# A pooled-attention and shrink kernel: order of loads, stores and last tokens on the queues, and the engine that places the turned keys, in groups 3 to 6

## The chip, the cores and the metric

One core of a Trainium2 chip. The metric is the time of one execution on the device, in microseconds (us). The kernel before takes 295.48 us as the median of three runs (294.96 to 295.68).

## The reference

Queries, keys and values are 8 batches x 8 heads x 576 tokens x 64. Keys and values are averaged over 8 neighbouring tokens, so that each head has 72 pooled keys. Each token's attention output goes, all heads side by side, through a two-layer block of width 512, 2048, 512.

```python
k_p = k.reshape(B, H, Sp, pool, D).mean(axis=3)
v_p = v.reshape(B, H, Sp, pool, D).mean(axis=3)
scores = scale * np.matmul(q, k_p.transpose(0, 1, 3, 2))
scores = scores - np.max(scores, axis=-1, keepdims=True)
attn = np.exp(scores)
attn = attn / (np.sum(attn, axis=-1, keepdims=True) + 1e-09)
attn_out = np.matmul(attn, v_p)
x = attn_out.transpose(0, 2, 1, 3).reshape(B * S, H * D)
h = x @ w_in
out = (h - np.tanh(h)) @ w_out
```

## The kernel before

**Tiling.** The 4608 tokens are worked on in nine groups of 512. Groups 0 to 7 are the first 512 tokens of batches 0 to 7. The last 64 tokens of each batch are gathered, two batches at a time, into four "tail" units, which together make group 8. While the two-layer block of group `g` runs, the attention of batch `nb = g + 1` is woven into it, and the loading and pooling for batch `nb + 1 = g + 2`.

**A group from 3 on** (`SEVEN`) has two stages. In the h stage TensorE multiplies by `w_in` into pairs of PSUM banks (`h_mms`, L445). ScalarE takes the tanh of a pair (L458) and VectorE subtracts it (L459, into `gT`); there are eight pairs. In the products stage the second multiplication is done by seven block products in place of eight (`product`, L591), for 14 steps `u` = 0 to 13. The operand of the third product, `S3`, is a VectorE difference of parts of `gT` (`g_sum`, L573), done in two halves at the end of the h stage. TensorE needs it at step u = 4. VectorE and GpSimd make the other sums (L573, L623, L624, L628), ScalarE and VectorE empty PSUM.

**The attention of the next batch** is placed by the table `PLAN7`: "s" are scores (`s_mms`, L311) with the maximum and the subtraction on VectorE (L323, L326), "e" the exponential on ScalarE (L362), "t" the turning of two units' exponentials by a transposing DMA (`e_turn_dma`, L371, into `ET`), "a" the values (`av_mms`, L398) and the normalising on VectorE (L419, L420), "x" the turning of the result into the next group's `xT` (L428). Keys -16 to -1 are steps of the h stage, keys from 0 on are the steps `u`. A tail's scores stand at u = 9.

**Preparation of the batch after.** GpSimd pools the values of batch `nb` (`pool_v`, L229 to L256), then the keys of batch `nb + 1` (`pool_k`, L214 to L220) at the start of a group. ScalarE casts its queries (`q_cast`, L280). `seven_more(u)` then issues on the SP queue the turning of the queries at u = 0 (`q_turn_dma`, L286) and of the keys at u = 7 (`k_turn_dma`, L272), the loading of a tail's queries at u = 7 when `nb` is even (`tail_pieces`, L176), and at u = 13 the placing of the turned keys into `KB` by GpSimd (`k_place_kT`, two copies at L266), the cast of the tail's queries by GpSimd (`tail_cast`, L184) and the loads of keys and queries of batch `g + 3` (`load_for`, L136, L142, L164). `KB` is read by the first scores of the next group. The tail's queries are turned (`turn_tail`, L187) behind the first "t" of the next group.

**Order on a queue.** Each engine, and SP with it, takes its instructions in the order of the program; semaphores make an instruction wait for what it depends on. SP issues nearly all DMAs from group 1 on, the transposing ones too. A half of a group's output is stored by `store_half` (L632): half 1 at u = 11, behind a GpSimd sum (`finish_22`, L628), half 0 at u = 13, so half 1 stands ahead of the loads on SP and half 0 behind them.

In the lines below `se` is ScalarE's copy and `ge` GpSimd's.

Of the kernel before, what the change touches and what calls it, by code (L numbers as in the profile page):

```python
# [38 lines left out]
def kernel(  # L39
# [130 lines left out]
    def run(pieces, n=16):  # L170
        for _ in range(min(n, len(pieces))):
            pieces.pop(0)()

    def tail_pieces(i, eng=None):
        return [
            lambda s=s: (eng or nc.sync).dma_start(  # L176
                out=tl_raw[64 * s : 64 * s + 64, :, :],
                in_=q[2 * i + s, :, QA:S, :].rearrange("h p d -> p h d"),
            )
            for s in range(2)  # L180
        ]

    def tail_cast(i):
        nc.gpsimd.tensor_copy(out=tl_bf[i % 2][:, :, :], in_=tl_raw[:, :, :])  # L184
# [737 lines left out]
        9: [("sb", 4, P45)],  # L922
        11: [("e", 4), ("t", 2)],
    }
    late, carry = [], []

    def tail_values(i):
        av_mms(slot_tl, av_tail(i), P67)
# [6 lines left out]
    for g in range(1, NG):  # L935
        nb = g + 1 if g + 1 < B else None
        more = nb is not None and nb + 1 < B

        tail = {2: 0, 3: 1, 5: 2, 7: 3}.get(nb)
        plan = {}  # L940
        if nb is not None:
            units = [(s_block(nb, j), av_block(nb), slot(4 * nb + j)) for j in range(4)]
            s_pairs, a_pairs = [0, 0, 0, 1, 2], [0, 1, 0, 2, 1]
            plan = {
                -12: [("s", 0)],
                -9: [("e", 0)],
                -8: [("s", 1)],
                -5: [("e", 1), ("t", 0)],
                -3: [("s", 2)],
                0: [("e", 2)],  # L950
                1: [("s", 3)],
                3: [("e", 3), ("t", 1)],
                4: [("a", 0)],
                5: [("a", 1), ("x", 0)],
                9: [("a", 2), ("a", 3), ("x", 1)],
            }
            if g == 1:
                plan[-10], plan[-7], plan[-5] = plan.pop(-12), plan.pop(-9), plan.pop(-8)
                plan[-2], plan[-1] = [("e", 1), ("t", 0)], plan.pop(-3)
            if tail is not None:  # L960
                units.append((s_tail(tail), av_tail(tail), slot_tl))
                plan[3].append(("s", 4))
                plan[4] += [("e", 4), ("t", 2)]
                if g == 1:
                    plan[6], plan[7] = plan[4][:1], plan.pop(5)
                    plan[4] = plan[4][1:]
                    plan[10] = plan.pop(9)
                plan[12] = [("a", 4), ("x", 2)]
            if g in SEVEN:
                plan = {u: its for u, its in PLAN7.items() if tail is not None or u < 9}  # L970
            xs = [x_pair(), x_pair(), x_tl]
        if nb is not None:
            pool_v(nb, nc.gpsimd)
        if more and g in SEVEN:
            pool_k(nb + 1, nc.gpsimd)
        shs = {}

        def seven_more(u):
            if u == 0:
                q_turn_dma(nb + 1)  # L980
            if u == 7:
                k_turn_dma(nb + 1)
                if nb % 2 == 0:
                    run(tail_pieces(nb // 2))
            if u == 13:
                k_place_kT(nb + 1, ge)
                if nb % 2 == 0:
                    tail_cast(nb // 2)
                load_for(g + 1)

        def step(kind, n, bk=None):
            if kind == "t2":
                e_turn_dma(units[2][2], n, n + 1)
                return
            if kind == "t":
                e_turn_dma(units[2 * n][2], 0, 2 if n < 2 else 1)
                if tail and n == 0:
                    turn_tail(tail)
                return
            if kind == "x":  # L1000
                x_turn_dma(xs[n], *((nb, 2 * n, 2) if n < 2 else (B, tail, 1)))
                return
            s, a, sl = units[n]
            if kind == "s" and bk:
                s_mms(s, bk)
                ng = s_max(bk)
                late.append(lambda: s_exp_heads(bk, ng, sl))
            elif kind in ("s", "sb"):
                bk = bk or PAIRS[s_pairs[n]]
                s_mms(s, bk)  # L1010
                shs[n] = s_shift(bk)
            elif kind == "e":
                s_exp(shs[n], sl)
            else:
                bk = bk or PAIRS[a_pairs[n]]
                av_mms(sl, a, bk)
                normalise(bk, xs[n // 2][:, n % 2, :, :, :])

        for i in range(NHID):
            bk = HB[i // 2 % 3][i % 2] if g in SEVEN else i % 6  # L1020
            h_mms(g, i, bk)
            if g in SEVEN and i == 15:
                for it in plan.pop(-1, ()):
                    step(*it)
            if i % 2:
                h_act(i - 1, bk - 1)
                if g in SEVEN:
                    if nb is None and i in (3, 5) and carry:
                        carry.pop(0)()
                    for n, i0 in {13: [(3, 0)], 15: [(3, 4)]}.get(i, ()):  # L1030
                        g_sum(n, i0, i0 + 4)
                    if i == 15 and nb is None:
                        for n in (2, 1):
                            g_sum(n, 0, NQ)
            for it in plan.get(i - NHID, ()):
                step(*it)
            if more and i in (13, 15):
                q_cast(nb + 1, se, i - 13, i - 11)
        v_next = v_pieces(nb + 1) if more else []
        if g > 1:  # L1040
            run(v_next)
        for u in range(14 if g in SEVEN else 0):
            n, b = PRODUCTS[u // 2], u % 2
            product(n, b)
            evacuate(n, b, nb is not None)
            for it in plan.get(u, ()):
                step(*it)
                run_late()
            if nb is not None and u in (9, 10) and carry:
                carry.pop(0)()  # L1050
            if more:
                seven_more(u)
            if nb is not None and u == 2:
                dep = g_sum(2, 0, NQ)
                after([g_sum(1, 0, 4, nc.gpsimd), g_sum(1, 4, NQ, nc.gpsimd)], dep)
            if u == (3 if nb is None else 8):
                g_sum(4, 0, NQ)
            if g == NG - 1:
                if n == "1" and b:
                    finish_11(nc.vector)  # L1060
                    store_part(0, C1, 0, 2)
                elif n == "6" and b:
                    store_part(1, C1, 0, 2)
                elif n == "5" and b:
                    store_part(1, C2, 0, 2, (nc.sync, nc.scalar))
                elif n == "3":
                    store_part(0, C2, b, b + 1, (nc.sync, nc.scalar))
            elif b:
                if n == "1":
                    finish_11(nc.gpsimd, nb is not None)  # L1070
                elif n in "53":
                    if n == "5" and nb is not None:
                        finish_22(nc.gpsimd)
                    store_half(g, 0 if n == "3" else 1)
        if g in SEVEN and tail is not None:
            carry += [lambda i=tail: tail_values(i), lambda i=tail: x_turn_dma(x_tl, B, i, 1)]
        for u, (tb, qd) in enumerate(() if g in SEVEN else UNITS):
            o_mms(tb, qd * 4, qd * 4 + 4, 4 + tb % 2)
            if qd == 3:
                o_store(g, tb, 4 + tb % 2, se)  # L1080
                if g == 1 or tb > 1:
                    run(stores)
            for it in plan.get(u, ()):
                step(*it)
            if u == 0 and more:
                pool_k(nb + 1, nc.gpsimd)
            if more:
                if u == (0 if g == 1 else 3):
                    q_turn_dma(nb + 1)
                if u == 0:  # L1090
                    run(stores)
                if u == (4 if g == 1 else 9):
                    k_turn_dma(nb + 1)
                    k_place_kT(nb + 1, ge)
                if u == 11 and nb % 2 == 0:
                    run(tail_pieces(nb // 2))
                    tail_cast(nb // 2)
            if u == 13:
                load_for(g + 1)
            if u in (8, 9, 13, 14):  # L1100
                w_ops.pop(0)()
# [29 lines left out]
```

## Time and profile before

| what | value |
|---|---|
| median of three runs | 295.48 us |
| the profiled execution's own time | 294.32 us |
| its span in the profile | 292.6 us |
| TensorE busy | 280.9 us, 96% of the span |
| VectorE busy | 222.0 us, 76% |
| GpSimd busy | 153.0 us, 52% |
| ScalarE busy | 147.4 us, 50% |
| granted TensorE clock | 1.0 throughout |

PE is the matmul side of TensorE, PEld its weight loads, DVE is VectorE, ACT ScalarE, POOL GpSimd. SPq stands for instructions that SP issues to the DMA queue. A busy sum of TensorE is an average over the whole span; what a stage can win is read from its waits. Groups 3 to 6 begin at 116.65, 145.46, 175.82 and 206.0 us of the span, group 7 at 235.32 us.

### The profile page before, as it was taken

The numbers are of one execution on the slowest core, as the hardware profiler recorded it, in microseconds if no ns is written. First come the engines' busy times: TensorE is split into PE (matmuls) and PEld (weight loads), VectorE is DVE, ScalarE is ACT, GpSimd is POOL, SyncE is SP. The second block draws the span as 40 slices with busy tenths as digits, with TensorE's granted clock in tenths as the row PEclk, the third lists the DMA queues.
The fourth block names the chain that finished last, engine by engine and source line by source line (L and its number), as shares of the span: only waits on it lengthen the run. The fifth ranks groups of instructions, "written<-read, shape, count | busy, mean of one in ns | idle before, by whom it ended". The sixth has DMA issues, their size and how long they took to land.

```text
span 292.6 us, 5473 instructions
## 1 busy us (share of the span) xinstructions
PE 280.9 (96%) x2154; PEld 179.0 (61%) x2163; DVE 222.0 (76%) x310; ACT 147.4 (50%) x220; POOL 153.0 (52%) x126
## 2 busy tenths in 40 slices
PE   7799999999999999999999899989999999999994
PEld 2489955444544455458845784478547854884583
DVE  6786876988848976699579976996599847935782
ACT  2786752466326831576257634773375336415630
POOL 7839871448512960982979589729840920010000
PEclk9999999999999999999999999999999999999999
DMA  7999999799999998887889968969623641011005
GB/s 229 228 285 273 205 275 219 151 307 299 228 230 275 299 245 197 278 224 209 146 237 265 258 145 249 281 197 165 197 43 62 78 166 21 0 72 76 0 2 143
DMA packets 84474, 54.56 MB, mean 186 GB/s; under 512 B 59904, under 2 KB 73344, under 8 KB 84448
## 3 DMA queue, kind: packets, MB, share of 16 engines
q1 hardware_dynamic: 77744, 45.17, 62.5%
q0 software_dynamic: 6320, 8.65, 14.1%
q10 hardware_dynamic: 384, 0.39, 0.5%
q8 instruction: 17, 0.28, 0.4%
q14 instruction: 9, 0.07, 0.1%
HBM read 36.70 MB, written 9.44 MB: 158 GB/s over the span
## 4 chain that ended last, share of the span: by engine, by line
PE 69%; DVE 20%; ACT 5%; DMA 3%; issue 1%; ACTq 0%; DVEq 0%
PE PS L445 24%; PE PS L591 20%; PE PS L513 14%; DVE gT L459 10%; PE PS L465 4%; PE PS L398 4%; DVE sh L326 3%; DVE mx L323 3%; PE PS L311 2%; ACT t_sb L458 2%; DMA ET<-E 2%; DVE q_raw L573 2%; DMA k_raw<-in_k_dram 1%; PE PS L292 1%; ACT ET L381 1%
## 5 line engine op out<-in xcount | busy, mean ns | idle before, releaser
L445 PE MATMUL PS<-xT,w1b 128*128 128x512 bf16 x448 | 100.8, 379 | 0.0
L459 DVE TENSOR_TENSOR gT<-PS,t_sb 128x1024 bf16<-128x1024 f32 x64 | 76.8, 1217 | 27.4 <-ACT t_sb L458 27.2
L458 ACT ACTIVATE t_sb<-PS 128x1024 f32<-128x1024 f32 x64 | 65.5, 1024 | 54.4 <-PE PS L445 53.0
L445 PEld LDWEIGHTS <-w1b 128*128 128x128 bf16 x512 | 49.4, 98 | 55.2 <-issue 0.3
L591 PEld LDWEIGHTS <-gT 128*128 128x128 bf16 x480 | 46.0, 98 | 5.8
L513 PE MATMUL PS<-w2b,gT 128*128 128x512 bf16 x183 | 44.7, 379 | 0.5
L591 PE MATMUL PS<-w2b,gT 128*128 128x256 bf16 x288 | 35.0, 272 | 0.0
L573 POOL TENSOR_TENSOR gT<-gT 128x1024 bf16<-128x1024 bf16 x8 | 16.8, 2119 | 25.9 <-DVE rden L419 25.9
L513 PEld LDWEIGHTS <-gT 128*128 128x128 bf16 x192 | 17.4, 98 | 17.4
L323 DVE TENSOR_REDUCE mx<-PS 128x8 f32<-128x576 f32 x35 | 26.1, 747 | 1.7 <-PE PS L311 1.7
L326 DVE TENSOR_TENSOR sh<-PS,mx 128x576 f32<-128x576 f32 x35 | 26.5, 757 | 1.2
L362 ACT ACTIVATE E<-sh 128x576 bf16<-128x576 f32 x31 | 21.1, 682 | 9.5 <-DVE sh L326 9.5
L420 DVE TENSOR_TENSOR x_sb<-PS,rden 128x512 bf16<-128x512 f32 x32 | 22.1, 691 | 1.1
L229 POOL TENSOR_TENSOR v_raw<-v_raw 128x1280 f32<-128x1280 f32 x6 | 17.4, 2893 | 7.5 <-DMA v_raw<-in_v_dram 7.3
L214 POOL TENSOR_TENSOR k_raw<-k_raw 128x1280 f32<-128x1280 f32 x6 | 17.4, 2901 | 6.3 <-DMA k_raw<-in_k_dram 5.5
L618 DVE TENSOR_TENSOR o_h<-PS,q_raw 128x256 f32<-128x256 f32 x20 | 8.5, 424 | 14.7 <-PE PS L591 12.5
L624 POOL TENSOR_TENSOR o_h<-o_h,k_raw 128x512 f32<-128x512 f32 x5 | 7.2, 1440 | 22.2 <-DVE o_h L618 21.9
L419 DVE RECIPROCAL rden<-PS 128x8 f32<-128x8 f32 x36 | 7.3, 203 | 12.9 <-PE PS L398 12.8
L398 PE MATMUL PS<-VB,ET 128*128 128x130 bf16 (+2 forms) x192 | 16.3, 221 | 0.8 <-DMA ET<-E 0.7
L535 ACT COPY o_h<-PS 128x512 f32<-128x512 f32 x10 | 5.7, 582 | 21.1 <-PE PS L513 21.1
L465 PE MATMUL PS<-xT,w1b 128*128 128x128 bf16 x256 | 15.6, 219 | 0.3 <-ACT xT L437 0.3
L398 PEld LDWEIGHTS <-ET 128*128 128x128 bf16 x192 | 13.3, 98 | 4.1 <-DMA ET<-E 1.1
(103 smaller groups left out, 372.0 us busy)
## 6 DMA issues: line engine op xcount, KB each, us to landing
k_raw<-in_k_dram SPq DMA_DIRECT2D x14, 512.0 KB, 7.3
q_raw<-in_q_dram SPq DMA_DIRECT2D x12, 512.0 KB, 7.4
v_raw<-in_v_dram SPq DMA_DIRECT2D x12, 512.0 KB, 5.0
out_dram<-o_h SPq DMA_DIRECT2D x10, 512.0 KB, 3.6
out_dram<-o_h SPq DMA_DIRECT2D x12, 256.0 KB, 2.9
w1b<-in_moe_w_in_dram POOLq DMA_DIRECT2D x4, 512.0 KB, 10.4
q_raw<-in_q_dram POOLq DMA_DIRECT2D x2, 1024.0 KB, 16.4
w2b<-in_moe_w_out_dram POOLq DMA_DIRECT2D x4, 512.0 KB, 11.4
```

Source lines behind the costliest of these rows:

```text
L323: nc.vector.reduce_max(out=mx.rearrange("p k h o -> p k (h o)"), in_=sc, axis=AX.X)
L326: nc.vector.tensor_tensor(out=sh[:, :, :, :], in0=sc, in1=mx.to_broadcast([128, 2, 4, G]), op=ALU.subtract)
L362: nc.scalar.activation(out=E[:, e, :, :].rearrange("p t c -> p (t c)")[:, 0:NK], in_=sh.rearrange("p k h c -> p (k h c)"), func=ACT.Exp, s ...
L398: nc.tensor.matmul(PS[ps, banks[half], D1 * h : D1 * (h + s1 - s0)], lhsT=ET[:, t, c0 : c0 + (ps.stop - ps.start)], rhs=VB[kb][:, t, s0:s1 ...
L420: nc.vector.tensor_tensor(out=x_sb, in0=ps[:, :, :, 0:D], in1=rden.to_broadcast([128, 2, 4, D]), op=ALU.mult,)
L445: nc.tensor.matmul(PS[:, bank, :].rearrange("p (j c) -> p j c", j=R), lhsT=w1b[:, fb, i * 128 : (i + 1) * 128], rhs=xT_of(g)[:, :, fb, :], ...
L458: nc.scalar.activation(out=t_sb[:, :, :], in_=ps, func=ACT.Tanh)
L459: nc.vector.tensor_sub(out=gT[:, i : i + 2, :], in0=ps, in1=t_sb[:, :, :])
L465: mm = nc.tensor.matmul(PS[:, bank, 128 * n : 128 * n + 128], lhsT=w1b[:, fb, (4 * c + n) * 128 : (4 * c + n + 1) * 128], rhs=xT_of(0)[:, ...
L513: mm = nc.tensor.matmul(PS[:, bank, 0 : c1 - c0], lhsT=gT[:, i, tb * 128 : (tb + 1) * 128], rhs=w2b[:, i, c0:c1], start=(i == 0), stop=(i ...
L573: return eng.tensor_tensor(out=o, in0=x, in1=y, op=op)
L591: nc.tensor.matmul(ps, lhsT=A[:, i, 128 * b : 128 * b + 128], rhs=B_[:, i, :], start=(n in "24" and i == 0), stop=(i == NQ - 1), skip_grou ...
```

## The change

The change touches `seven_more`, `step` and the loop over groups.

- The two copies that place the turned keys go from GpSimd to ScalarE (end of groups 3, 4 and 5).
- In groups 3, 4 and 5 the store of half 1 is held in a list and issued at u = 13 behind the loads for the batch after. With the store of half 0 it then stands behind the loads on SP. (In group 5 there are no loads left.)
- A tail's queries are loaded behind both stores at the end of groups 3 and 5, in place of at u = 7.
- They are cast on GpSimd in the next group (4 and 6), behind the pooling of values and keys, in place of ahead of it.
- They are turned behind the second "t" of that group (u = 0), in place of the first one (step -7 of the h stage).

Nothing is added or removed in count: the same copies, casts, loads, stores and transposing DMAs are there.

```diff
-    late, carry = [], []
+    late, carry, held = [], [], []
...
             pool_v(nb, nc.gpsimd)
         if more and g in SEVEN:
             pool_k(nb + 1, nc.gpsimd)
+        if nb in (5, 7):
+            tail_cast(tail)
         shs = {}
 
         def seven_more(u):
...
             if u == 7:
                 k_turn_dma(nb + 1)
-                if nb % 2 == 0:
-                    run(tail_pieces(nb // 2))
             if u == 13:
-                k_place_kT(nb + 1, ge)
-                if nb % 2 == 0:
-                    tail_cast(nb // 2)
+                k_place_kT(nb + 1, se)
                 load_for(g + 1)
+                while held:
+                    held.pop(0)()
...
                 e_turn_dma(units[2 * n][2], 0, 2 if n < 2 else 1)
-                if tail and n == 0:
+                if tail and n == (1 if g in SEVEN else 0):
                     turn_tail(tail)
...
                     if n == "5" and nb is not None:
                         finish_22(nc.gpsimd)
+                    if more and n == "5":
+
+                        held.append(lambda g=g: store_half(g, 1))
+                        continue
                     store_half(g, 0 if n == "3" else 1)
+                    if n == "3" and more and nb % 2 == 0:
+                        run(tail_pieces(nb // 2))
```

## The prediction

> **What bounds the kernel now.** First the page's head, then the busy time by group.
>
> ```profile
> span 292.6 us, 5473 instructions
> PE 280.9 (96%) x2154; PEld 179.0 (61%) x2163; DVE 222.0 (76%) x310; ACT 147.4 (50%) x220; POOL 153.0 (52%) x126
> ```
>
> TensorE is the bound. The windows of groups 4 and 5 (length, then PE, PEld, DVE, ACT and POOL busy) show how little there is to win:
>
> ```profile
> 145.46:175.82 30.36, 29.42 (x225) 19.67 (x224) 24.91 (x32) 16.91 (x26) 24.37 (x17) 1.00 0.96 221
> 175.82:206.00 30.18, 29.40 (x230) 19.97 (x228) 24.44 (x32) 16.36 (x25) 22.76 (x16) 1.00 0.89 221
> ```
>
> 30.36 - 29.42 = 0.94 us of group 4 and 30.18 - 29.40 = 0.78 us of group 5 are idle. TensorE's timeline names the waits (the last one is group 6's):
>
> ```profile
> 164.92 1.48 PE L591 MATMUL PS<-v_raw,q_raw 128*128 128x256 bf16 x12 [0.24 <-DVE q_raw L573]
> 168.34 0.53 PE L398 MATMUL PS<-VB,ET 128*128 128x130 bf16 x6 [0.70 <-DMA ET<-E]
> 195.71 1.48 PE L591 MATMUL PS<-v_raw,q_raw 128*128 128x256 bf16 x12 [0.78 <-DVE q_raw L573]
> 225.29 1.48 PE L591 MATMUL PS<-v_raw,q_raw 128*128 128x256 bf16 x12 [0.20 <-DVE q_raw L573]
> ```
>
> 0.24 + 0.70 + 0.78 + 0.20 = 1.92 us is all that the change can win from TensorE's waits in its groups. Three are waits for the second half of S3 (L573), one is for turned exponentials. What stands behind S3 is in the chain of waits:
>
> ```profile
> 175.82 1.74 PE PS L445 x8
> 177.65 1.03 ACT t_sb L458
> 178.77 1.23 DVE gT L459
> ...
> 194.96 0.70 DVE q_raw L573
> ```
>
> From 178.77 to 195.66 the chain stays on VectorE but for gaps of some hundredths, 16.9 us. So two things move TensorE's wait at u = 4 one for one: the end of the group's first tanh, and anything that lengthens a VectorE instruction before S3.
>
> **The change part by part.** The sum is made against the profiled execution (294.32 us, span 292.6, so 1.72 us outside the span); the median of the runs is 295.48, that is 1.16 more, and the forecast is given on the median's scale.
>
> *Loads ahead of the store (group 4's end), worth 0.59 us in group 5.* The first half of S3, the same instruction in groups 4, 5 and 6 (VectorE's timeline):
>
> ```profile
> 160.76 0.80 DVE L573 TENSOR_TENSOR q_raw<-gT 128x1024 bf16<-128x1024 bf16 x1
> 191.06 1.27 DVE L573 TENSOR_TENSOR q_raw<-gT 128x1024 bf16<-128x1024 bf16 x1
> 221.24 0.68 DVE L573 TENSOR_TENSOR q_raw<-gT 128x1024 bf16<-128x1024 bf16 x1
> ```
>
> In group 6, which pools no keys, it takes 0.68. In group 5 it takes 1.27, and GpSimd's timeline shows why:
>
> ```profile
> 182.29 1.79 POOL L256 TENSOR_TENSOR VB<-v_raw,mask 128x960 bf16<-128x960 f32 x1
> 185.62 2.91 POOL L214 TENSOR_TENSOR k_raw<-k_raw 128x1280 f32<-128x1280 f32 x1 [1.54 <-DMA k_raw<-in_k_dram]
> ...
> 190.23 1.55 POOL L220 TENSOR_TENSOR kd<-k_raw 128x640 bf16<-128x640 f32 x1
> ```
>
> L220 ends at 191.78, and L573 at 192.33, 0.55 later: it hardly moved until GpSimd had finished. 1.27 - 0.68 = 0.59 us is lost there. GpSimd is that late because it waited 1.54 us for keys. On SP the keys' loads stood behind the store of half 1 (group 4's end, SP's timeline, then size and landing of the keys' loads there):
>
> ```profile
> 176.39 0.53 SPq L632 DMA_DIRECT2D out_dram<-o_h  x1
> 176.98 1.34 SPq L136 DMA_DIRECT2D k_raw<-in_k_dram  x2
> ```
>
> ```profile
> k_raw<-in_k_dram SPq DMA_DIRECT2D x2, 512.0 KB, 6.8
> ```
>
> With the store behind them the loads are issued 176.98 - 176.39 = 0.59 earlier and have the store's 512 KB (as much as one of these loads: 128 x 1024 floats) less in front. At 221 GB/s (group 4's window) that is 2.4 us, so the keys come 0.6 to 3.0 us earlier; GpSimd is free for them at 182.29 + 1.79 = 184.08. L214 to L220 took 191.78 - 185.62 = 6.16. Started between 184.08 and 185.0 they end between 190.2 and 191.2. Against 191.06 that clears the whole block, or leaves 0.1. I take 0.59; bounds 0 (keys no earlier) and 0.59. The wait of 0.78 would be 0.19, close to group 6's 0.20.
>
> *Keys placed by ScalarE, end of groups 3, 4 and 5.* GpSimd loses 0.90 us of work per group, ScalarE gains two copies. No such copy on ScalarE is in the trace; its nearest copies by form are
>
> ```profile
> L611 ACT COPY o_h<-PS 128x256 f32<-128x256 f32 x16 | 6.0, 372 | 13.5 <-PE PS L591 13.5
> L604 ACT COPY k_raw<-PS 128x512 f32<-128x512 f32 x6 | 3.5, 586 | 2.8 <-PE PS L591 2.8
> ```
>
> For 288 elements I take 0.39 each, 0.78 for both (bounds 0.74 and 1.17, twice either row). By the Trainium skill's "ScalarE: Activation LUTs", section "What ACT_TABLE_LOAD costs", 186 ns + 0.833 ns an element less 93 ns of overlap would give 0.76 for both, an estimate, and the sum would be 0.02 lower.
>
> They are hidden if they end before the next group's first tanh, which is queued right behind them on ScalarE. Here the end of group 3 matters (SP, GpSimd and ScalarE timelines):
>
> ```profile
> 142.54 1.23 SPq L272 DMA_TRANSPOSE kT<-kd  x1
> ...
> 146.97 1.37 SPq L136 DMA_DIRECT2D k_raw<-in_k_dram  x2
> ```
>
> ```profile
> 144.93 1.26 POOL L628 TENSOR_TENSOR o_h<-o_h,q_raw 128x512 f32<-128x512 f32 x1
> 147.07 0.90 POOL L266 COPY KB<-kT 64x288 bf16<-64x288 bf16 x2 [0.88 <-DMA kT<-kd]
> 148.54 0.61 POOL L184 CAST tl_bf<-tl_raw 128x512 bf16<-128x512 f32 x1 [0.57 <-POOL KB L266]
> 149.11 2.89 POOL L229 TENSOR_TENSOR v_raw<-v_raw 128x1280 f32<-128x1280 f32 x1
> ```
>
> ```profile
> 147.28 1.02 ACT L458 ACTIVATE t_sb<-PS 128x1024 f32<-128x1024 f32 x1 [3.16 <-PE PS L445]
> ```
>
> The turned keys arrived at 147.07, only 0.21 before the tanh. If they do so again, the copies end at 147.07 + 0.78 = 147.85 and the tanh is 0.57 late, and with it everything on VectorE up to S3. Why 147.07? The landing of the keys' turning at the end of group 3, then of the two turnings at the end of group 4, and the queue of instruction fetches between 144.4 and 145.2:
>
> ```profile
> kT<-kd SPq DMA_TRANSPOSE x1, 4.5
> ```
>
> ```profile
> xT<-x_sb SPq DMA_TRANSPOSE x1, 2.7
> kT<-kd SPq DMA_TRANSPOSE x1, 2.6
> ```
>
> ```profile
> q8 instruction: 1, 0.02, 9.2%
> ```
>
> 4.5 us against 2.6, and a fetch of instructions falls on its end. The change moves neither the turning nor TensorE's program, so I take 147.07 again: +0.57. Bounds: 0 (landing after 2.6, at 145.2) and 0.96 (copies of 1.17). At the end of group 4 there is room:
>
> ```profile
> 163.75 1.51 SPq L371 DMA_TRANSPOSE ET<-E  x1
> ...
> 172.42 1.23 SPq L272 DMA_TRANSPOSE kT<-kd  x1
> ```
>
> 172.42 + 2.6 = 175.0, and 1.3 us later where the tail's turning now stands in front; copies to 177.1, before the tanh at 177.65. The same 1.3 also lies ahead of the queries' turning and of xT, which the next group needs at 175.82; the second xT, the DMA just ahead of 172.42, lands 2.7 us after an issue at about 171.2, so it has 1.9 us to spare. I take 0 for both; without that cover each tenth would count in full.
>
> *Tail's cast and GpSimd's earlier start, group 4.* Group 4's pooling now begins when L628 ends, at 146.19, in place of 149.11, 2.92 earlier. It ended with
>
> ```profile
> 161.08 1.87 POOL L220 TENSOR_TENSOR kd<-k_raw 128x640 bf16<-128x640 f32 x1
> ```
>
> at 162.95, so it will at 160.03; with the cast (0.61) GpSimd is done by 160.7, where S3's first half began at 160.76, or 161.3 if the tanh is late. The 0.80 there becomes 0.68: 0.12 won.  If the cast came late (its load now stands behind loads and both stores), it could hold S3 by up to its 0.61. The Trainium skill's "SBUF — State Buffer", section "Who interferes with whom", says that a VectorE instruction with two SBUF inputs and a GpSimd instruction that reads SBUF lock each other out for a whole instruction, whichever comes first. The 0.55 above agrees; by it the moved cast is a new candidate, worth up to 0.61, where the sum has 0.
>
> *Exponentials' wait of 0.70, group 4.* The turning of units 2 and 3 was issued at 163.75; its landing and the queues at that time:
>
> ```profile
> q8 instruction: 1, 0.02, 5.4%
> ...
> ET<-E SPq DMA_TRANSPOSE x1, 4.5
> ```
>
> The tail's turning now follows it and no longer delays the values' loads that stand ahead. But a fetch of instructions falls into it as well, at a place of TensorE's program that the change leaves alone, so I let the 0.70 stand; bounds 0 and 0.70 won. The tail's turned queries are needed first at u = 9, behind the values of units 2 and 3 that begin at 168.34.
>
> *Sum.* Group 5: -0.59. Group 4: +0.57 - 0.12 = +0.45, in u = 4 and in the exponentials' wait alike, since both hang on VectorE's chain; counted once. Group 6: 0. Together -0.14 us: 294.2 for the profiled execution, **295.3** for the median.
>
> **The rivals.**
>
> *The keys' turning lands in time (295.48 - 0.59 - 0.12 = 294.8).* For it: 2.6 us at group 4's end, and the tail's load no longer follows it. Against: the fetch stays.
>
> *The exponentials' wait goes too.* If loads that run three microseconds earlier let that turning finish before the fetch, 0.70 more: 294.1 with the keys in time, 294.6 if not. For it: the values' loads ahead of it move up by the tail's 1.3 us. Against: the fetch.
>
> *The loads hold up the turned keys: slower.* At the end of group 3, 2 MB of loads now start right behind the keys' turning, at 143.8 in place of 146.97. Group 4's first turned exponentials, which ran beside loads, landed after
>
> ```profile
> ET<-E SPq DMA_TRANSPOSE x1, 5.6
> ```
>
> At 5.6 us the keys land at 148.14, 1.07 later; the tanh is 1.64 late and TensorE waits for its scores as well. -0.14 + 1.07 = +0.9: 296.4; from 5.6 us on it is slower beyond the measurement. Against it: the turning is in front on its queue.
>
> *The change wins nothing:* the keys come no earlier, 295.9 with the late tanh.
>
> **How the numbers follow.** Forecast 0.33 (295.3); keys in time 0.19 (294.8); exponentials too 0.25 (294.1 to 294.6); loads hold the keys 0.17 (296.4 and up); nothing won 0.06. A measurement can tell 0.3% from no change, 0.9 us: below 294.6 is faster, above 296.4 slower. Faster: the exponentials' case, and half of the keys in time, 0.34. Slower 0.17, the rest 0.49. The range goes from 293.9 (all of 1.92 would be 293.6) to 296.5; the forecast's own is 294.7 to 295.9.
>
> **What would show it.** Right: group 5's first S3 half at 0.68 and its wait near 0.2; ScalarE's copies ending some 0.6 past the tanh's old place in group 4, and TensorE's wait at u = 4 there grown to about 0.7. Wrong: in group 4 a tanh on time; GpSimd still waiting for keys in group 5; no wait for exponentials; a late xT at a group's start.

## The result and the profile after

| kernel | median, us | runs | lowest to highest |
|---|---|---|---|
| before | 295.44 | 12 | 294.68 to 296.13 |
| changed | 294.28 | 12 | 293.75 to 295.46 |

The ratio is 0.9966, with a 95% interval of 0.9951 to 0.9981: 1.0 us faster by the ratio (0.6 to 1.4). Two more sets of the changed kernel, each beside the kernel before on its own chip, gave 0.9961 (0.9941 to 0.9981) and 0.9975 (0.9954 to 0.9996). The time lies in the range that was given (293.9 to 296.5), but below the likeliest case's own range (294.7 to 295.9).

The profiled execution took 294.34 us, nearly the same as that of before (294.32), with the same span. The page's head:

```profile
span 292.6 us, 5472 instructions
PE 281.2 (96%) x2154; PEld 179.1 (61%) x2163; DVE 221.5 (76%) x310; ACT 150.5 (51%) x226; POOL 149.0 (51%) x120
```

Six instructions have left GpSimd for ScalarE (the copies of three groups, two each). Groups 4 and 5 in the windows (length, then PE, PEld, DVE, ACT, POOL busy, granted clock, DMA share, GB/s):

```profile
146.16:176.56 30.40, 29.50 (x226) 19.66 (x224) 25.14 (x32) 18.22 (x29) 23.12 (x15) 1.00 0.86 221
176.56:206.15 29.59, 29.39 (x230) 20.03 (x228) 23.86 (x32) 17.98 (x29) 21.94 (x13) 1.00 0.87 225
```

Group 5 went from 30.18 to 29.59, group 4 from 30.36 to 30.40. TensorE's timeline, with the same four waits as before (groups 4, 4, 5 and 6):

```profile
166.07 1.48 PE L591 MATMUL PS<-v_raw,q_raw 128*128 128x256 bf16 x12 [0.60 <-DVE q_raw L573]
169.07 0.53 PE L398 MATMUL PS<-VB,ET 128*128 128x130 bf16 x6 [0.29 <-DMA ET<-E]
195.86 1.48 PE L591 MATMUL PS<-v_raw,q_raw 128*128 128x256 bf16 x12 [0.20 <-DVE q_raw L573]
225.45 1.48 PE L591 MATMUL PS<-v_raw,q_raw 128*128 128x256 bf16 x12 [0.20 <-DVE q_raw L573]
```

0.24 became 0.60, 0.70 became 0.29, 0.78 became 0.20. Behind them stand the first halves of S3 on VectorE (groups 4 and 5),

```profile
162.01 0.68 DVE L573 TENSOR_TENSOR q_raw<-gT 128x1024 bf16<-128x1024 bf16 x1
191.81 0.68 DVE L573 TENSOR_TENSOR q_raw<-gT 128x1024 bf16<-128x1024 bf16 x1
```

GpSimd's last sums and the cast,

```profile
158.76 1.54 POOL L220 TENSOR_TENSOR kd<-k_raw 128x640 bf16<-128x640 f32 x1
160.25 0.60 POOL L184 CAST tl_bf<-tl_raw 128x512 bf16<-128x512 f32 x1
...
184.67 2.91 POOL L214 TENSOR_TENSOR k_raw<-k_raw 128x1280 f32<-128x1280 f32 x1 [0.81 <-DMA k_raw<-in_k_dram]
189.28 1.55 POOL L220 TENSOR_TENSOR kd<-k_raw 128x640 bf16<-128x640 f32 x1
```

and the copies on ScalarE ahead of group 4's first tanh:

```profile
147.70 0.88 ACT L266 COPY KB<-kT 64x288 bf16<-64x288 bf16 x2 [2.87 <-DMA kT<-kd]
148.60 1.03 ACT L458 ACTIVATE t_sb<-PS 128x1024 f32<-128x1024 f32 x1
```

In both groups GpSimd is done (160.85 and 190.83) before VectorE begins S3, so both halves take 0.68. The tanh has no wait of its own any more: it starts where the copies end.

One profile of each kernel doesn't carry a difference of tenths, so each kernel was profiled three times. Below, a group is counted from TensorE's first row of L445 to the next group's (that row starts some 0.16 us ahead of the bounds of the windows shown so far); "tanh" is the start of group 4's first tanh from there, and the last two columns are the wait at u = 4 and for exponentials, both in group 4.

| profile | group 2 | group 4 | group 5 | tanh | u = 4 | exponentials |
|---|---|---|---|---|---|---|
| before | 31.30 | 30.37 | 30.18 | 1.99 | 0.24 | 0.70 |
| before, second (b1) | 32.09 | 29.86 | 30.46 | 1.98 | 0.30 | 0.24 |
| before, third (b2) | 32.15 | 30.74 | 29.88 | 1.99 | 0.36 | 0.83 |
| changed | 31.46 | 30.40 | 29.59 | 2.60 | 0.60 | 0.29 |
| changed, second (e4) | 31.29 | 29.98 | 29.60 | 2.65 | 0.60 | none |
| changed, third (e10) | 31.30 | 30.45 | 29.59 | 2.71 | 0.60 | 0.25 |

The means of groups 4 and 5 together are 60.50 before and 59.87 after: 0.63 us less, of which group 5 has 0.58 and group 4 0.05. Groups 3 and 6 are the same to 0.06. Single profiles of one kernel lie up to 0.9 apart in group 4, so its 0.05 is no change. The other 0.4 us or so of the measured gain is not in the groups that the change touches; group 2, ahead of all that was changed, is 0.50 shorter on the mean (31.85 to 31.35).

### The profile page after: what moved, and what is told of

It reads as the page before. It is cut to its first block, busy times and chain, and to the rows that moved or that the text cites. A ratio compares the mean times of both kernels' runs of the same rounds, so it can differ in the third digit from the quotient of the medians.

```text
span 292.6 us, 5472 instructions
## 1 busy us (share of the span) xinstructions
PE 281.2 (96%) x2154; PEld 179.1 (61%) x2163; DVE 221.5 (76%) x310; ACT 150.5 (51%) x226; POOL 149.0 (51%) x120
## 4 chain that ended last, share of the span: by engine, by line
PE 59%; DVE 22%; DMA 9%; ACT 4%; POOL 2%; SPq 2%; issue 2%; ACTq 0%; POOLq 0%; DVEq 0%
PE PS L591 19%; PE PS L445 17%; DVE gT L459 12%; PE PS L513 12%; DMA v_raw<-in_v_dram 5%; DVE sh L326 4%; PE PS L465 4%; PE PS L398 4%; DVE mx L323 4%; ACT t_sb L458 2%; DVE q_raw L573 2%; PE PS L311 1%; DMA ET<-E 1%; DMA tl_T<-tl_bf 1%; DMA k_raw<-in_k_dram 1%
## 5 line engine op out<-in xcount | busy, mean ns | idle before, releaser
L445 PE MATMUL PS<-xT,w1b 128*128 128x512 bf16 x448 | 100.8, 379 | 0.0
L445 PEld LDWEIGHTS <-w1b 128*128 128x128 bf16 x512 | 49.4, 98 | 55.2
L573 POOL TENSOR_TENSOR gT<-gT 128x1024 bf16<-128x1024 bf16 x8 | 16.8, 2121 | 31.6 <-DVE rden L419 31.6
L326 DVE TENSOR_TENSOR sh<-PS,mx 128x576 f32<-128x576 f32 x35 | 26.5, 757 | 1.2
```

Source lines behind the costliest of these rows:

```text
L326: nc.vector.tensor_tensor(out=sh[:, :, :, :], in0=sc, in1=mx.to_broadcast([128, 2, 4, G]), op=ALU.subtract)
L445: nc.tensor.matmul(PS[:, bank, :].rearrange("p (j c) -> p j c", j=R), lhsT=w1b[:, fb, i * 128 : (i + 1) * 128], rhs=xT_of(g)[:, :, fb, :], ...
L573: return eng.tensor_tensor(out=o, in0=x, in1=y, op=op)
```

## The experiments

All times; the ratio is to the kernel before, run on the same chip.

| run | what it is | median, us (runs) | ratio, 95% | group 4 | group 5 |
|---|---|---|---|---|---|
| e1_place | before + copies on ScalarE | 295.20 (12) | 0.9986, 0.9967 to 1.0006 | 31.36 | 29.78 |
| e2_loads | before + loads ahead of the store | 294.38 (12) | 0.9966, 0.9941 to 0.9990 | 30.42 | 29.60 |
| e3_tail | before + tail later | 295.04 (12) | 0.9982, 0.9960 to 1.0004 | 30.19 | 30.07 |
| e4_after | changed kernel | 294.32 (12) | 0.9961, 0.9941 to 0.9981 | 29.98 | 29.60 |
| b1_before | kernel before | 296.08 (1) | | 29.86 | 30.46 |
| e5_noplace | changed, copies on GpSimd | 294.11 (12) | 0.9961, 0.9944 to 0.9979 | 30.01 | 29.59 |
| e6_early | changed, keys turned at u = 0 | 293.80 (12) | 0.9954, 0.9937 to 0.9970 | 29.88 | 29.60 |
| e7_pad32 | changed, 32 matmuls more at the start | 296.39 (10) | 1.0034, 1.0013 to 1.0055 | 29.32 | 29.97 |
| e9_early3 | changed, keys turned at u = 0 in group 3 alone | 293.54 (6) | 0.9943, 0.9923 to 0.9964 | 29.63 | 29.59 |
| e10_after | changed kernel | 294.66 (12) | 0.9975, 0.9954 to 0.9996 | 30.45 | 29.59 |
| b2_before | kernel before | 295.83 (1) | | 30.74 | 29.88 |

### Each part alone: copies, loads, tail

**The copies alone.**

```diff
-                k_place_kT(nb + 1, ge)
+                k_place_kT(nb + 1, se)
```

> Only the placing of the turned keys goes to ScalarE; loads, stores and tails stay as before. Theory (the first tanh of group 4 sets VectorE's chain, and the turned keys land at about 147 because an instruction fetch falls on their end): the two copies stand in front of group 4's first tanh, which starts 0.5 to 0.7 us later from the group's start than before (1.82 us there), and TensorE's wait for S3 in group 4 grows from 0.24 to about 0.7; group 5 keeps its wait of about 0.8, since its keys come no earlier. Total 0.0 to +0.5 us. Rival (freeing GpSimd is what gains): group 5's wait falls to 0.2 and the total to -0.5.

VectorE's, GpSimd's and TensorE's timelines in group 4 (the last line is group 5's):

```profile
162.22 1.86 DVE L573 TENSOR_TENSOR q_raw<-gT 128x1024 bf16<-128x1024 bf16 x1
```

```profile
149.34 0.61 POOL L184 CAST tl_bf<-tl_raw 128x512 bf16<-128x512 f32 x1 [2.23 <-DMA tl_raw<-in_q_dram]
...
162.00 1.54 POOL L220 TENSOR_TENSOR kd<-k_raw 128x640 bf16<-128x640 f32 x1
```

```profile
165.69 0.52 PE L398 MATMUL PS<-VB,ET 128*128 128x130 bf16 x6 [0.81 <-DVE sh L326]
...
167.46 1.48 PE L591 MATMUL PS<-v_raw,q_raw 128*128 128x256 bf16 x12 [0.82 <-DVE q_raw L573]
...
197.20 1.48 PE L591 MATMUL PS<-v_raw,q_raw 128*128 128x256 bf16 x12 [0.39 <-DVE q_raw L573]
```

The tanh is late as in the whole change (2.62), but here GpSimd still has the tail's cast ahead of its pooling and waits 2.23 us for the tail's queries, and its last sum meets S3: 162.00 + 1.54 = 163.54, and S3 ends at 162.22 + 1.86 = 164.08, 0.54 later. TensorE pays twice: 0.81 for a subtraction of scores that VectorE does behind S3's first half (L326), and 0.82 at u = 4. Group 4 is the longest of all, 31.36. So the late tanh costs little only because the other parts have got GpSimd out of the way. In group 5, where no change was expected, the wait is 0.39 and not 0.8; this is one profile, and the third one of before, below, has 0.48. In time this part can't be told from the kernel before.

**The loads alone.**

```diff
-    late, carry = [], []
+    late, carry, held = [], [], []
...
                 load_for(g + 1)
+                while held:
+                    held.pop(0)()
...
+                    if more and n == "5":
+                        held.append(lambda g=g: store_half(g, 1))
+                        continue
                     store_half(g, 0 if n == "3" else 1)
```

> Only the store of half 1 goes behind the loads; placing and tails stay as before. Theory (keys that come earlier take GpSimd's last sum off the first half of S3): in group 5 the first half of S3 takes 0.68 in place of 1.27 and the wait falls from 0.78 to about 0.2; group 4 unchanged. Total -0.4 to -0.7 us, that is the whole gain seen in the profile. Rival (the gain is the tail's move, or GpSimd's freed time): group 5 keeps 0.5 or more of its wait, total within 0.2.

GpSimd's, VectorE's and TensorE's timelines, groups 4 and 5:

```profile
161.55 1.54 POOL L220 TENSOR_TENSOR kd<-k_raw 128x640 bf16<-128x640 f32 x1
...
185.57 2.91 POOL L214 TENSOR_TENSOR k_raw<-k_raw 128x1280 f32<-128x1280 f32 x1
```

```profile
161.88 1.76 DVE L573 TENSOR_TENSOR q_raw<-gT 128x1024 bf16<-128x1024 bf16 x1
...
192.31 0.68 DVE L573 TENSOR_TENSOR q_raw<-gT 128x1024 bf16<-128x1024 bf16 x1
```

```profile
167.02 1.48 PE L591 MATMUL PS<-v_raw,q_raw 128*128 128x256 bf16 x12 [0.81 <-DVE q_raw L573]
...
196.37 1.48 PE L591 MATMUL PS<-v_raw,q_raw 128*128 128x256 bf16 x12 [0.20 <-DVE q_raw L573]
```

In group 5 the pooling begins without a wait, S3 takes 0.68 and TensorE waits 0.20: the whole of group 5's gain, from this part alone (29.60). In group 4 the opposite: GpSimd's sums now end right when S3 begins (163.09; S3 ends 163.64), and the wait grows from 0.24 to 0.81, where no change was expected. Its ratio is that of the whole change.

**The tail alone.**

```diff
+        if nb in (5, 7):
+            tail_cast(tail)
...
-                if nb % 2 == 0:
-                    run(tail_pieces(nb // 2))
...
-                if nb % 2 == 0:
-                    tail_cast(nb // 2)
...
-                if tail and n == 0:
+                if tail and n == (1 if g in SEVEN else 0):
                     turn_tail(tail)
...
                     store_half(g, 0 if n == "3" else 1)
+                    if n == "3" and more and nb % 2 == 0:
+                        run(tail_pieces(nb // 2))
```

> Only the tail's load, cast and turning move; placing stays on GpSimd and the store stays ahead of the loads. Theory: the values' loads of group 4 no longer stand behind the tail's turning, so the wait for exponentials falls from 0.70 to 0.3 to 0.5 and group 4 is 0.2 to 0.4 shorter than before, group 5 keeps 0.78. Total -0.1 to -0.5 us. Rival (an instruction fetch alone makes that wait): 0.70 stays, total within 0.2.

VectorE and GpSimd in group 4:

```profile
162.50 1.23 DVE L573 TENSOR_TENSOR q_raw<-gT 128x1024 bf16<-128x1024 bf16 x1
```

```profile
161.63 1.55 POOL L220 TENSOR_TENSOR kd<-k_raw 128x640 bf16<-128x640 f32 x1
163.12 1.08 POOL L184 CAST tl_bf<-tl_raw 128x512 bf16<-128x512 f32 x1
```

S3 meets the sum again (163.18, and 0.55 later 163.73), then the cast that has been put behind it waits for VectorE in its turn: 1.08 in place of 0.60. The prediction had the cast holding S3 by up to 0.61; here the cast is the one held, by 0.48. TensorE's wait at u = 4 was 0.74. Its wait for exponentials was 0.15, less than the 0.3 to 0.5 expected, but TensorE also came to them later; group 4 as a whole is 30.19, within what the kernel before shows. In time this part, too, can't be told from no change.

**The changed kernel again**, beside these three:

> The changed kernel as it is, beside its parts on one chip. Theory: its gain is the sum of the three parts within 0.3 us, with group 4's late tanh (+0.45) inside it: -0.6 to -1.2 us. Rival (the parts interact, for instance the tail's cast only fits when ScalarE places the keys): the sum of the parts is off by 0.5 or more.

Group 5 is 29.60 and the tanh at 2.65, as in the first profile; the wait for exponentials is gone altogether (the turning landed after 3.7 us). Do the parts add up? Groups 4 and 5 together are 0.64 longer in e1, 0.48 shorter in e2 and 0.24 shorter in e3 than the mean of before (60.50), a sum of -0.08, where the whole change has -0.63. That speaks for parts that help each other, as the lines of e1 show, but each part has one profile only. In time the parts' gains come to 0.66% against 0.39% of the whole, with intervals too wide to tell these apart.

### Is group 4's late tanh a loss, and what makes the turnings late?

**The changed kernel with the copies back on GpSimd**, where they stand ahead of the pooling:

```diff
-                k_place_kT(nb + 1, se)
+                k_place_kT(nb + 1, ge)
```

> The changed kernel with the turned keys placed by GpSimd again; loads, stores and tails as changed. Theory: group 4's first tanh is on time (1.99 from the first matmul, in place of 2.60), but GpSimd waits for the turned keys and its pooling ends 1 us or more later, at 16 from the group's start, so S3's first half (due at 15.4) is held behind its last sum: 1.2 to 1.9 long. TensorE's wait in group 4 is 0.6 to 1.3, the kernel 0.0 to +0.7 us against the changed one. Rival (the late tanh costs more than GpSimd's time): group 4 is 0.4 shorter, the kernel 0.4 faster than the changed one.

TensorE, VectorE and GpSimd in group 4:

```profile
165.67 1.48 PE L591 MATMUL PS<-v_raw,q_raw 128*128 128x256 bf16 x12 [0.59 <-DVE q_raw L573]
```

```profile
161.21 1.08 DVE L573 TENSOR_TENSOR q_raw<-gT 128x1024 bf16<-128x1024 bf16 x1
```

```profile
160.19 1.56 POOL L220 TENSOR_TENSOR kd<-k_raw 128x640 bf16<-128x640 f32 x1
161.68 1.08 POOL L184 CAST tl_bf<-tl_raw 128x512 bf16<-128x512 f32 x1
```

The tanh is on time (1.99), but GpSimd starts later and S3 is held: 1.08. The wait at u = 4 is 0.59 against 0.60. The placing on ScalarE pays 0.6 at the tanh and gets 0.4 back at S3, and between the times there is no difference that the intervals show.

**The keys turned early.** In e6 the turning moves to u = 0 in all groups, in e9 in group 3 alone:

```diff
                 q_turn_dma(nb + 1)
-            if u == 7:
+            if u == (0 if nb == 4 else 7):
                 k_turn_dma(nb + 1)
```

> The changed kernel with the keys' turning issued at u = 0, right behind the queries' turning, in place of u = 7. Theory: the turned keys land some 4 us ahead of the group's end, ScalarE does not wait for them, group 4's first tanh is at 1.99 and S3's wait in group 4 falls from 0.60 to 0.2; group 4 is 0.3 to 0.5 shorter, the kernel 0.3 to 0.5 us faster than the changed one. Rival: the turning of the results for the next group's h stage, now behind it on SP, comes late and the next group starts later: slower by up to 1 us. Second rival (VectorE's chain has slack at its start): no change.

> The changed kernel with the keys' turning issued at u = 0 in group 3 alone, where an instruction fetch falls on it; groups 4 and 5 issue it at u = 7. Theory: group 4's first tanh on time, its S3 wait 0.2, and group 5 begins without the small gap that the run with every turning at u = 0 had; group 4 is 29.5 to 29.8 long, the kernel 0.3 to 0.6 us faster than the changed one. Rival (that gap had another cause): 29.9 again, same as with every turning early.

ScalarE in e6, then TensorE and the window of group 4 in e9:

```profile
144.82 0.88 ACT L266 COPY KB<-kT 64x288 bf16<-64x288 bf16 x2
...
148.08 1.02 ACT L458 ACTIVATE t_sb<-PS 128x1024 f32<-128x1024 f32 x1 [2.38 <-PE PS L445]
```

```profile
165.42 1.48 PE L591 MATMUL PS<-v_raw,q_raw 128*128 128x256 bf16 x12 [0.19 <-DVE q_raw L573]
```

```profile
145.97:175.60 29.63, 29.30 (x227) 19.66 (x224) 25.30 (x32) 17.12 (x26) 23.11 (x14) 1.00 0.85 222
```

The copies no longer wait, the tanh is on time (1.99 in both), S3 begins with GpSimd done, and the wait at u = 4 is 0.18 and 0.19. That shows the turned keys' landing as the cause of the late tanh, and the cost of it: group 4 is 29.63 in e9 against 30.40, 29.98 and 30.45. e9 is faster than the kernel before by 0.9943 (0.9923 to 0.9964), while the changed kernel beside it on the same chip had 0.9975; the two intervals overlap. In e6 the turning of the next x stands behind the keys' in group 4 too, and group 4 won less (29.88); why was not taken apart.

**A shift of TensorE's program.** 32 matmuls of zeros into an unused bank, at the start; everything after them is fetched at other moments:

```diff
     fill(11, 7)
+    fill(32, 7, 8)
```

> The changed kernel with 32 tiny matmuls more at the very start, which do nothing but move all that follows by 64 instructions in TensorE's program. They cost 0 to 2 us ahead of group 1; what counts is group 4. Theory (an instruction fetch of TensorE that falls on a transposing DMA makes it late): the fetches that fell at the end of group 3 and on the exponentials of group 4 come some 5 us earlier in their groups; the keys' turning lands after 2.6 in place of 4.4, group 4's first tanh is at 1.99, its S3 wait 0.2, and no wait for exponentials. Group 4 29.5 to 29.7 long in place of 30.0 to 30.4. Rival (the turnings are late because of the other DMAs beside them): landing after 4.4 again, group 4 unchanged.

The landings of keys (group 3's end), of exponentials in group 4, and of exponentials in group 6 with the fetch beside them:

```profile
kT<-kd SPq DMA_TRANSPOSE x1, 3.0
...
ET<-E SPq DMA_TRANSPOSE x1, 3.4
...
q8 instruction: 1, 0.02, 1.8%
...
ET<-E SPq DMA_TRANSPOSE x1, 5.0
```

```profile
167.11 1.48 PE L591 MATMUL PS<-v_raw,q_raw 128*128 128x256 bf16 x12 [0.19 <-DVE q_raw L573]
...
230.23 0.53 PE L398 MATMUL PS<-VB,ET 128*128 128x130 bf16 x6 [1.11 <-DMA ET<-E]
```

Groups 3 to 6 hold the same instructions, yet the keys land after 3.0 in place of 4.4 to 4.5 us, the tanh is on time (2.00), the exponentials land after 3.4 and nobody waits for them: group 4 takes 29.32. Group 6, 29.32 to 29.33 in every other profile, now has a fetch on its exponentials, a wait of 1.11 and 30.61. The lateness goes where the fetch goes. Group 5 has a fetch on its second exponentials now, and they land after 4.0 in place of 3.5. The kernel as a whole is slower, and not by the added matmuls themselves: group 1 begins at 54.0, as elsewhere (53.5 to 54.7), but takes 33.5 us in place of 31.6 to 32.1.

### Two more profiles of the kernel before, one more set of the changed one

These ask whether the first profile of before stands for its kernel.

> The kernel before once more, for one more profile. Theory (the profile shown of before was a lucky one: in group 4 S3's first half arrived between two GpSimd sums and was held for 0.12 only): here it is held longer, 1.1 to 1.9 us in place of 0.80, and TensorE's wait for S3 in group 4 is 0.5 to 1.3 in place of 0.24; group 5 again 1.1 to 1.3 and 0.6 to 0.8. Rival (that profile was typical): 0.8 and 0.24 again, and the larger gain of the timed runs lies elsewhere, ahead of group 3 for instance.

> The kernel before a third time. Theory: groups 4 and 5 together take 60.3 to 60.6 us as in the two profiles so far, against 59.6 to 60.0 of the changed kernel; what the timed runs gain beyond that is not in these groups. Rival (the profiles so far were low): 61 or more, with S3's first half in group 4 held until GpSimd's last sum ends.

> The changed kernel once more, on the same chip as the kernel with the early turning, and for a further profile of groups 4 and 5. Theory: group 4 30.0 to 30.4 long with the tanh at 2.6, group 5 29.6; 0.9 to 1.3 us faster than before in time. Rival (its first measurement was high by chance): 0.5 or less.

TensorE's timeline of the third profile of before:

```profile
111.31 0.89 PE L398 MATMUL PS<-VB,ET 128*128 128x130 bf16 x12 [0.68 <-DMA ET<-E]
...
166.68 1.49 PE L591 MATMUL PS<-v_raw,q_raw 128*128 128x256 bf16 x12 [0.36 <-DVE q_raw L573]
...
170.22 0.53 PE L398 MATMUL PS<-VB,ET 128*128 128x130 bf16 x6 [0.83 <-DMA ET<-E]
...
197.29 1.48 PE L591 MATMUL PS<-v_raw,q_raw 128*128 128x256 bf16 x12 [0.48 <-DVE q_raw L573]
```

Groups 4 and 5 of before are no accident: 60.55, 60.32 and 60.62 together, and S3's first half in group 4, which the theory of b1 had at 1.1 to 1.9, took 0.82 in b1 and 0.90 in b2. Group 2 differs: its exponentials, issued 19.9 us after its start in every profile, landed after 3.5 us in the first and after 5.5 in b1 and b2, with a wait of 0.62 and 0.68 that the first one hasn't. In b1 and b2 a fetch (queue q8) falls on that transfer, some 23.0 us after the group's start; in the first profile it comes at 23.7, just behind the landing at 23.5. A group 2 of 32.1 to 32.2 is in four of the five profiles of kernels that store ahead of the loads (b1, b2, e1 and e3; e3 waits at the tail's scores there), and in none of the eight that store behind them (31.3 to 31.5, e6 31.84, also at the tail's scores). But group 2 lies ahead of the first instruction that the change touches. Why the fetch should come earlier in one kernel than in the other is open; it may be chance.

## Why the prediction was right, and where it wasn't

The time lies in the range, but the range spans 2.6 us, from nearly all that could be won to the slower rival. The likeliest case, 295.3, was missed by 1.0 us, and a time below 294.6 had been given a chance of 0.34. The three parts of the change came out in size; the term for the exponentials' wait was wrong, and some 0.4 us of the gain lies where the sum had nothing.

**Loads ahead of the store: right, and in its size.** Group 5's half of S3 went from 1.27 to 0.68 and its wait from 0.78 to 0.20; the forecast was 0.59, the mean of three against three is 0.58. The pooling of keys began 8.27 us after the group's start in place of 9.96, so 1.7 earlier (the bounds were 0.6 to 3.0). GpSimd still waits 0.81 for keys, which the prediction had named as a sign of being wrong; the block was gone anyway. e2 shows that this part does it alone.

**Keys placed by ScalarE: right.** The two copies took 0.88 (estimate 0.78, inside the bounds), the keys landed 4.4 us after their issue (4.5 before), and the tanh moved by 0.61 (forecast 0.57). TensorE's wait at u = 4 is 0.60, where about 0.7 was expected.

**Cast and GpSimd's earlier start: right.** L220 took 1.54 in place of 1.87, the half of S3 0.68 in place of 0.80, and the cast fitted in between. e1 shows what this was worth: without it the late tanh falls on GpSimd's last sum.

**The exponentials' wait: the step that failed.** The sum counted +0.45 for group 4 "in u = 4 and in the exponentials' wait alike, since both hang on VectorE's chain". At u = 4 it came: the product begins 20.07 us after TensorE's first row of the group in place of 19.63, 0.44 later. The issue of the exponentials' turning moved with it, but its landing did not. From TensorE's first row of the group, with the fetch (queue q8) found in stretches of a quarter us and the landing as issue plus duration:

| profile | issued | fetch at | landed after | so at | wait |
|---|---|---|---|---|---|
| before | 18.46 | 19.5 | 4.5 | 23.0 | 0.70 |
| b1 | 18.41 | 19.25 | 4.1 | 22.5 | 0.24 |
| b2 | 18.70 | 20.0 | 4.7 | 23.4 | 0.83 |
| changed | 18.90 | 19.25 | 4.1 | 23.0 | 0.29 |
| e4 | 18.95 | 19.5 | 3.7 | 22.7 | none |
| e10 | 19.00 | 20.0 | 4.1 | 23.1 | 0.25 |
| e7 | 18.32 | 17.5 | 3.4 | 21.7 | none |

Over the three profiles of each kernel the issue is 0.43 later on the mean (18.52 to 18.95), the fetch is where it was (19.6 in both), and so is the landing (23.0 and 22.9). That the fetch is what held the landing in place is argued and not shown: other DMAs beside the turning moved as well, and in e6 and e9 the issue (18.3), the fetch (between 18.5 and 18.9) and the landing (22.3) all come earlier together. The rows on SP and on the DMA queues for the changed kernel:

```profile
164.90 2.26 SPq L371 DMA_TRANSPOSE ET<-E  x1
```

```profile
q8 instruction: 1, 0.02, 5.3%
...
ET<-E SPq DMA_TRANSPOSE x1, 4.1
```

TensorE, 0.44 later from u = 4 on, finds less to wait for, and begins the values at 23.07 in place of 23.05. So the term at the exponentials is -0.41 (0.70 to 0.29; by the three profiles each, 0.59 to 0.18), not zero. In this pair of profiles that leaves +0.44 - 0.41 = +0.03 for group 4 in place of +0.45 (30.37 to 30.40), and by the three of each -0.05. With group 5's -0.58 that is the -0.63 of the windows. The prediction had a rival in which this wait goes, 294.6 with the keys late, and that came nearest, but for another reason: it had the turning finish before the fetch, by an earlier issue, and the issue came later.

**What the sum had no term for.** 0.63 in groups 4 and 5 is the low end of what was measured (0.6 to 1.4 us). The median of before, 1.1 us above its profiled execution, was carried over as a constant; b1 and b2 show that some 0.8 of it can be a wait in group 2 that the first profile happened not to have. Whether the changed kernel meets it less often is not settled; if it does not, this part of the gain is luck.

**The slower rival** (loads hold up the turned keys, 5.6 us) didn't come: 4.4 us.

## What to carry to other kernels

A wait for a DMA need not move with its issue: look for what falls on its landing before you add a delay to every wait behind it, and remember that two waits one after the other on one engine share their time. Edits that each cost something alone (a late tanh, a cast put behind a sum) can be free together, when one takes away what the other would run into; so cost the order on each engine as a whole. Before tenths are argued about, take the kernel before in several profiles, and cut them by region.

## What the runs showed of the hardware

**An instruction fetch delays a transposing DMA in flight.** The keys' turning took 4.2 to 4.6 us with a fetch (queue q8, 16 KB) on its end, 3.0 when the fetch was moved (e7), and 2.6 at group 4's end of the kernel before. The exponentials' in group 4 took 3.7 to 4.7 with it and 3.4 without; where e7 had moved it to, they took 4.0 (group 5) and 5.0 (group 6), against 3.4 to 3.5 there in the changed kernel. In all profiles but e7's the exponentials of group 4 landed 3.0 to 3.6 us after the fetch and 3.7 to 4.7 after their issue. In the first profile of before, the fetch stands between 164.75 and 165.00; the queue of the turning moves 208 packets in the quarter of a us from 165.25, then 100, 3, 1, 8, 9 and 9, and 219 from 167.00 on. In e7, with no fetch on the transfer, it moves 188 to 232 in every quarter from 167.30 to 169.30. So the transfer stops for over a microsecond behind the fetch; why one fetch of 16 KB does that, the trace doesn't show.

**VectorE and GpSimd shut each other out in both directions.** Whenever S3's first half began under GpSimd's last sum it ended 0.54 to 0.55 us after that sum (group 4 of e1, e2, e3 and e5, group 5 of before, b1, b2, e1 and e3), however long that made it: 0.68 by itself, up to 1.86. Where VectorE came first, GpSimd's sum took 1.87 in place of 1.54 and the cast 1.08 in place of 0.60. That is what the Trainium skill says in "SBUF — State Buffer", section "Who interferes with whom"; the price was these runs' to show.
